# The last addition of each weight conversion: a VectorE instruction replaced by an accumulating transfer that GpSimd issues

## The chip, the cores and the metric

One Trainium2 chip, one core. The metric is the device time of one execution in microseconds (us); lower is better. Besides the times there is a profile: one execution recorded by the hardware profiler. Its engine names are PE (TensorE matmuls), PEld (TensorE weight loads), DVE (VectorE), ACT (ScalarE), POOL (GpSimd) and SP (the queue that issues the kernel's transfers). A line such as L265 is line 265 of the kernel.

## The reference

A gated linear attention over 4 batches, 8 heads, 768 steps and head size 48 keeps a 48x48 state for each head; its output, as 3072 tokens of 384 numbers, goes through a feed-forward layer with 2048 hidden units.

```python
for t in range(S):
    state = alpha[:, :, t, :, None] * state + np.einsum('bhd,bhe->bhde', k[:, :, t], v[:, :, t])
    y[:, :, t] = np.einsum('bhd,bhde->bhe', q[:, :, t], state)
...
h = x @ w_in
g = np.maximum(0.01 * h, h)
return (g @ w_out).astype(np.float32)
```

The weights `w_in` (384x2048) and `w_out` (2048x384) arrive as 64-bit floating point numbers. No engine of the kernel works on those directly; the kernel receives them as 64-bit integers and builds from the bits two 32-bit parts of each weight, HIGH and LOW, whose sum is the weight.

## The kernel before, in words

**Tiling.** The tokens are cut into 24 units of 128 (one batch, 128 steps each); three units make a block of 384 tokens, so there are 8 blocks. The hidden layer is cut into 16 slices f of 128 units. For a block i and a slice f, `ffn_in` (line 485) makes the hidden values with nine matmuls of 128x384 at line 493: for each of three groups of the model dimension HIGH with the high and the low part of the tokens, then LOW with the high part. In a slice the third of the nine matmuls is thus the first that reads LOW weights. ScalarE scales the result by 0.01 (L496), VectorE takes the maximum (L499), ScalarE rounds it (L501) and VectorE subtracts to get the low part (L505). `ffn_out` (line 511) adds to the output with nine more matmuls at L520, three items later (LAG = 3).

**Stages.** First the attention for units 0 to 8, which are blocks 0 to 2 (scans on VectorE, L314 and L320; masks on GpSimd, L367; scalings of the state on GpSimd, L373). Then the feed-forward of blocks 0 and 1, interleaved slice by slice: (block 0, f), (block 1, f), and in the same stretch the weights are converted. From block 2 on the converted weights stay in SBUF, and the rest of the attention is spread between the matmuls.

**Weight conversion.** `load_weights` (L201) loads one slice of both weight matrices into one of four tiles `raw` (128 rows, 768 numbers of 64 bits): one transfer for `w_out` (L213) and four for `w_in` (L209), all issued by SP. `converting(f)` (L226) is a generator that makes HIGH and LOW of slice f in steps, so that its instructions can be placed between others:

- ScalarE scales the top words in place (L245); VectorE shifts and masks them (L248) and joins the sign (L251): the weight cut to 32 bits, in tile `bits`, also called `val` (two buffers).
- ScalarE rounds `val` to the matmul format: HIGH (L254).
- VectorE cuts the power of two out of `bits` into tile `pw` (L258, one buffer), subtracts HIGH from `val` in place (L260), multiplies the low word by 2**-52 and by the power, in place in `pw` (L262), and adds the two into LOW (L265).

**Order.** The program is built by a scheduler that follows dependencies and a simulated timeline and fixes the order of the instructions on each engine's queue; the kernel pins places with "issue after" conditions. Slices 0, 1 and 2 are converted during the attention stage at pinned places. For slices 3 to 15, `put` (L217) fixes one order for VectorE and one for ScalarE across the feed-forward and the conversion: in slice f of block 0 come L248 of slice f+2, then the last step of slice f+1 (L265), then L251 of f+2; around block 1's maximum come L258, L260 and, after L505, L262 of f+2. So the conversion of f+2 is finished during slice f+1.

```python
coming = converting(f + SOON, True)
...
old, new, coming = new or iter(()), coming, converting(f + SOON + 1, True)
gs[n] = ffn_in(i, f, ((), (coming, new, old, new)))
...
gs[n] = ffn_in(i, f, ((new, new), (new,)))
next(new, None)
```

Here `old`, `new` and `coming` are the conversions of slices f+1, f+2 and f+3; each mention is one step. GpSimd issues no transfers in this kernel.

Of the kernel before, what the change touches and what calls it, by code (L numbers as in the profile page):

```python
# [9 lines left out]
F32 = mybir.dt.float32  # L10
F32R = mybir.dt.float32r
I32 = mybir.dt.int32
U32 = mybir.dt.uint32
I64 = mybir.dt.int64
AF = mybir.ActivationFunctionType
ALU = mybir.AluOpType
# [6 lines left out]
def gated_linear_attn_ffn(ctx, tc, q, k, v, alpha, w_in, w_out, out):  # L23
    nc = tc.nc
# [64 lines left out]
    state, vals_sb, rest = rest[:B], rest[B:B + NV], rest[B + NV:]  # L89
# [14 lines left out]
    made = {}  # L104
# [3 lines left out]
    def behind(*key):  # L108

        return tc.issue_after(made[key].ins) if key in made else nullcontext()  # L110
# [106 lines left out]
    def put(ordered, eng, op, *args):  # L217

        if not ordered:
            return op(*args)  # L220
        line = lines[eng]
        with tc.issue_after(line[-1].ins) if line else nullcontext():
            line.append(op(*args))
        return line[-1]

    def converting(f, ordered=False):  # L226

        if f >= NF:
            return
        raw = jobs.pop(f)  # L230
        w_sb[f] = cst.tile([P, 2, 2 * DM], F32R, name=f"w{f}")
        hi, lo = w_sb[f][:, HIGH, :], w_sb[f][:, LOW, :]
        if not f64:
            val = raw[:, :, 0:P].bitcast(F32)
            hi, lo = (t.rearrange("p (g f) -> p g f", f=P) for t in (hi, lo))
            nc.scalar.copy(hi, val)
            made["w", f] = nc.vector.tensor_tensor(lo, val, hi.bitcast(F32), ALU.subtract)
            return
        words = raw.rearrange("p g (f w) -> p (g f) w", w=2)
        top, low = words[:, :, 1], words[:, :, 0]  # L240
        bits = cvp.tile([P, 2 * DM], I32, name="bits", bufs=NBITS)
        val = bits.bitcast(F32)

        with nullcontext() if lines["ACT"] else behind(*AFTER.get(f, ("hi", f - 1))):
            put(ordered, "ACT", lambda: nc.scalar.mul(top.bitcast(F32), top.bitcast(F32), 2.0 ** -112))  # L245
        yield
        with nullcontext() if lines["ACT"] else behind("w", f - 1):
            put(ordered, "DVE", lambda: nc.vector.tensor_scalar(  # L248
                bits, top, 3, 0x7FFFFFF8, ALU.logical_shift_left, ALU.bitwise_and))
        yield  # L250
        put(ordered, "DVE", lambda: nc.vector.scalar_tensor_tensor(  # L251
            bits, top, -0x80000000, bits, ALU.bitwise_and, ALU.bitwise_or))
        yield
        made["hi", f] = put(ordered, "ACT", lambda: nc.scalar.copy(hi, val))  # L254
        yield
        pw = cvp.tile([P, 2 * DM], I32, name="pw", bufs=NPW)
        rest = pw.bitcast(F32)
        put(ordered, "DVE", lambda: nc.vector.tensor_scalar(pw, bits, -0x800000, None, ALU.bitwise_and))  # L258
        yield
        put(ordered, "DVE", lambda: nc.vector.tensor_tensor(val, val, hi.bitcast(F32), ALU.subtract))  # L260
        yield
        put(ordered, "DVE", lambda: nc.vector.scalar_tensor_tensor(  # L262
            rest, low.bitcast(U32), 2.0 ** -52, rest, ALU.mult, ALU.mult))
        yield
        made["w", f] = put(ordered, "DVE", lambda: nc.vector.tensor_tensor(lo, rest, val, ALU.add))  # L265

    def convert(f):
        for _ in converting(f):
            pass
# [284 lines left out]
    for n, _ in enumerate(st):  # L554
        if n == 2:
            load_values(NV - 1)
        while LOADS and LOADS[0][0] in made:
            key, f, part = LOADS.pop(0)
# [8 lines left out]
        if n in STARTS:  # L567
            i, f = items[len(gs)][:2]
# [8 lines left out]
    for n in range(len(items) + LAG):  # L577
        slices = 0
        if n < len(items):
            i, f, slices, _ = items[n]  # L580
            if f == 0:
                if i == 2:
                    st, held = attention(AHEAD, NU), HELD
                while i not in ready:
                    next(st)
                emitted, due = 0, 0.0
            if loaded_f < NF:
                load_weights(loaded_f)
                loaded_f += 1
                if loaded_f == NF:  # L590
                    asked, later = later, None
                    with behind("raw", NF - 1):
                        for fn, *args in asked:
                            fn(*args)
            if n < len(STARTS):
                pass
            elif i == 0:
                if coming is None:
                    coming = converting(f + SOON, True)
                    next(coming)  # L600
                old, new, coming = new or iter(()), coming, converting(f + SOON + 1, True)
                gs[n] = ffn_in(i, f, ((), (coming, new, old, new)))
            elif i == 1:
                gs[n] = ffn_in(i, f, ((new, new), (new,)))
                next(new, None)
            else:
                gs[n] = ffn_in(i, f)
        for half in range(2):
# [5 lines left out]
            if half == 0 and n >= LAG:  # L614
                i, f, _, tag = items[n - LAG]
# [130 lines left out]
```

## Time and profile before

| | |
|---|---|
| Three runs | 530.29, 530.71, 530.88 us; median 530.71 |
| Profiled execution, span from first to last instruction | 530.9 us (no other time of this execution is recorded) |
| Mean granted TensorE clock | 0.994 |
| L265, the last addition | 16 instructions, 15.4 us busy, 960 ns each |
| L262, the multiplication before it | 16 instructions, 15.7 us busy, 978 ns each |
| DMA engines, share of the span | 39.5% in the queue that SP issues to |

How to read the profile: the busy time of an engine is an average over stages with different limits. The "chain of work that ended last" is followed back from the last instruction, at each step to what released it. The view by stage gives the busy time of each engine in a stretch of the span. In the order of time, each line has the start and the length in us, the engine, the line, the operation with its output and inputs and how many instructions were merged, and in brackets the idle time before it with what ended it. A line on transfers gives their number, their size and the median time from issue to landing.

### The profile page before, as it was taken

The numbers are of one execution on the slowest core, as the hardware profiler recorded it, in microseconds if no ns is written. First come the engines' busy times: TensorE is split into PE (matmuls) and PEld (weight loads), VectorE is DVE, ScalarE is ACT, GpSimd is POOL, SyncE is SP. The second block draws the span as 40 slices with busy tenths as digits, with TensorE's granted clock in tenths as the row PEclk, the third lists the DMA queues.
The fourth block names the chain that finished last, engine by engine and source line by source line (L and its number), as shares of the span: only waits on it lengthen the run. The fifth ranks groups of instructions, "written<-read, shape, count | busy, mean of one in ns | idle before, by whom it ended". The sixth has DMA issues, their size and how long they took to land.

```text
span 530.9 us, 9962 instructions
## 1 busy us (share of the span) xinstructions
PE 518.5 (98%) x3778; PEld 500.0 (94%) x3778; DVE 379.0 (71%) x695; ACT 230.7 (43%) x489; POOL 62.6 (12%) x143
## 2 busy tenths in 40 slices
PE   8997999999999999999999999999999999999995
PEld 7886999999999999999999999999999999999995
DVE  6998899999999997777577586585786534333331
ACT  2764855555534444444334444345344444333331
POOL 4554500000000111100101101101010000000000
PEclk9998999999999999999999999999999999999998
DMA  9999975545726533552251431433201000101001
GB/s 144 168 175 170 229 172 133 131 122 141 170 45 184 127 84 81 102 134 49 60 111 30 112 83 44 92 74 86 54 15 25 31 16 1 23 1 44 1 0 51
DMA packets 92982, 46.64 MB, mean 88 GB/s; under 512 B 57856, under 2 KB 90112, under 8 KB 92928
## 3 DMA queue, kind: packets, MB, share of 16 engines
q1 hardware_dynamic: 92928, 45.93, 39.5%
q8 instruction: 32, 0.52, 0.4%
q14 instruction: 22, 0.18, 0.1%
HBM read 38.83 MB, written 4.72 MB: 82 GB/s over the span
## 4 chain that ended last, share of the span: by engine, by line
PE 87%; DVE 7%; DMA 4%; issue 1%; SPq 0%; DVEq 0%; ACT 0%
PE ph L493 35%; PE b L520 32%; PE a L356 4%; PE a L401 3%; PE a L520 3%; DMA small<-in_v_dram 3%; PE a L395 3%; PE a L412 2%; PE b L401 1%; PE a L380 1%; PE b L280 1%; DMA small<-in_alpha_dram 1%; DVE pw L262 1%; DVE gl L505 1%; DVE t L499 1%
## 5 line engine op out<-in xcount | busy, mean ns | idle before, releaser
L493 PE MATMUL ph<-large,w 128*128 128x384 f32 x1152 | 226.6, 338 | 0.5 <-DVE t L499 0.5
L493 PEld LDWEIGHTS ph<-large,w 128*128 128x128 f32 x1152 | 200.1, 188 | 2.8 <-DVE t L499 1.1
L520 PE MATMUL b<-w,gh 128*128 128x384 f32 x672 | 168.9, 340 | 0.0
L499 DVE TENSOR_TENSOR t<-ph,t 128x384 f32<-128x384 f32 x128 | 70.7, 553 | 79.1 <-ACT t L496 78.9
L520 PEld LDWEIGHTS b<-w,gh 128*128 128x128 f32 x672 | 119.4, 188 | 2.1 <-issue 0.4
L496 ACT ACTIVATE t<-ph 128x384 f32<-128x384 f32 x128 | 62.5, 489 | 128.2 <-PE ph L493 128.2
L501 ACT CAST gh<-t 128x384 fp32r<-128x384 f32 x128 | 65.7, 513 | 119.6 <-DVE t L499 119.6
L520 PE MATMUL b<-w,gl 128*128 128x384 f32 x336 | 107.4, 335 | 0.0
L505 DVE TENSOR_TENSOR gl<-t,gh 128x384 fp32r<-128x384 f32 x128 | 70.9, 554 | 34.3 <-ACT gh L501 34.2
L520 PEld LDWEIGHTS b<-w,gl 128*128 128x128 f32 x336 | 62.6, 188 | 0.0
L367 POOL TENSOR_SCALAR_AFFINE_SELECT sm<-sm 128x512 f32<-128x512 f32 x33 | 23.1, 712 | 207.8 <-ACT sm L366 207.8
L356 PEld LDWEIGHTS a<-qs,ks 48*128 48x128 f32 x312 | 24.1, 188 | 5.1 <-issue 4.2
L356 PE MATMUL a<-qs,ks 48*128 48x128 f32 x312 | 28.7, 285 | 0.0
L289 DVE STREAM_TRANSPOSE ks<-small 128x512 f32<-128x512 f32 x15 | 16.7, 1123 | 14.6 <-PE a L380 14.6
L324 POOL COPY pe<-pc 128x4 f32<-128x4 f32 x24 | 4.8, 202 | 163.7 <-DVE pc L314 163.7
L373 POOL TENSOR_TENSOR small<-us,pe 48x192 f32<-48x192 f32 x40 | 22.4, 560 | 1.5
L314 DVE TENSOR_TENSOR_SCAN pc<-e,small 128x128 f32<-128x128 f32 x60 | 20.4, 401 | 0.0
L366 ACT COPY sm<-a 128x512 f32<-128x512 f32 x24 | 14.0, 583 | 14.0 <-PE b L356 12.9
L520 PE MATMUL a<-w,gh 128*128 128x384 f32 x96 | 19.6, 337 | 0.0
L320 DVE TENSOR_TENSOR_SCAN rc<-e,small 128x511 f32<-128x511 f32 x15 | 19.1, 1276 | 0.2
L401 PE MATMUL a<-sm,small 128*48 128x128 f32 x256 | 17.7, 277 | 0.0
L254 ACT CAST w<-bits 128x768 fp32r<-128x768 f32 x16 | 13.4, 838 | 8.4 <-DVE bits L251 7.8
(92 smaller groups left out, 554.4 us busy)
## 6 DMA issues: line engine op xcount, KB each, us to landing
raw<-in_moe_w_out_dram SPq DMA_DIRECT2D x16, 384.0 KB, 3.8
small<-in_v_dram SPq DMA_DIRECT2D x24, 192.0 KB, 3.7
raw<-in_moe_w_in_dram SPq DMA_DIRECT2D x32, 144.0 KB, 4.0
out_dram<-o SPq DMA_DIRECT2D x24, 192.0 KB, 2.0
small<-in_alpha_dram SPq DMA_DIRECT2D x32, 96.0 KB, 2.3
small<-in_q_dram SPq DMA_DIRECT2D x30, 96.0 KB, 2.4
small<-in_k_dram SPq DMA_DIRECT2D x30, 96.0 KB, 2.2
small<-in_alpha_dram SPq DMA_DIRECT2D x30, 80.0 KB, 2.4
```

What stands on the lines that cost most here:

```text
L314: nc.vector.tensor_tensor_scan(pc[:, p, :], aT[:, p, :], ones.broadcast_to([P, C]), 1.0, ALU.mult, ALU.mult)
L320: nc.vector.tensor_tensor_scan(flat[2][:, NP * C - 2::-1], flat[0][:, NP * C - 1:0:-1], flat[1][:, NP * C - 2::-1], last, ALU.mult, ALU.add)
L356: nc.tensor.matmul(ss[s][:, p, :], ks[lo:lo + D, p, :], qs[lo:lo + D, p, :], start=True, stop=True)
L367: made["mask", u] = nc.gpsimd.affine_select(out=sm[s], in_=sm[s], compare_op=ALU.is_ge, fill=0.0, base=0, pattern=[[0, NP], [1, C]], chann ...
L373: nc.gpsimd.tensor_tensor(*scalings.pop(0))
L401: nc.tensor.matmul(y[lo:lo + m, p, :], V[:, c:c + m], masked[u][s][:, p, :], start=not tb and p == 0, stop=p == NP - 1, skip_group_check=True,
L493: nc.tensor.matmul(ph, w_in_of(f, wn, g), xt[:, g, :], start=n == 0, stop=n == 3 * NG - 1)
L496: put(ordered, "ACT", lambda: nc.scalar.mul(t, ph, 0.01))
L499: put(ordered, "DVE", lambda: nc.vector.tensor_tensor(t, ph, t, ALU.max))
L501: put(ordered, "ACT", lambda: nc.scalar.copy(gh, t))
L505: made["gl", i, f] = put(ordered, "DVE", lambda: nc.vector.tensor_tensor(gl, t, gh.bitcast(F32), ALU.subtract))
L520: product = nc.tensor.matmul(po[j], gt[:, js], w_out_of(f, wn), start=f == 0 and n == 0, stop=f == NF - 1 and n == 2)
```

## The change

The last VectorE instruction of the conversion goes. The subtraction writes LOW directly, the multiplication writes into `val`, and a transfer issued by GpSimd adds `val` (in SBUF) to LOW (in SBUF): 128 rows of 768 numbers of 32 bits, 384 KB. The two last VectorE instructions of the conversion keep their shapes but for their output tiles. The generator has one step less; the last step now holds the multiplication and the issue of the transfer, so in the fixed order both come where L262 stood, and the place of L265 stays empty. `made["w", f]`, by which slices 1 and 2 start behind the conversion before, now means the multiplication. That the transfer waits for the multiplication, and the LOW matmuls for the transfer, the scheduler finds from the tiles.

```diff
@@ -254,15 +254,14 @@
         made["hi", f] = put(ordered, "ACT", lambda: nc.scalar.copy(hi, val))
         yield
         pw = cvp.tile([P, 2 * DM], I32, name="pw", bufs=NPW)
-        rest = pw.bitcast(F32)
+        power = pw.bitcast(F32)
         put(ordered, "DVE", lambda: nc.vector.tensor_scalar(pw, bits, -0x800000, None, ALU.bitwise_and))
         yield
-        put(ordered, "DVE", lambda: nc.vector.tensor_tensor(val, val, hi.bitcast(F32), ALU.subtract))
+        put(ordered, "DVE", lambda: nc.vector.tensor_tensor(lo, val, hi.bitcast(F32), ALU.subtract))
         yield
-        put(ordered, "DVE", lambda: nc.vector.scalar_tensor_tensor(
-            rest, low.bitcast(U32), 2.0 ** -52, rest, ALU.mult, ALU.mult))
-        yield
-        made["w", f] = put(ordered, "DVE", lambda: nc.vector.tensor_tensor(lo, rest, val, ALU.add))
+        made["w", f] = put(ordered, "DVE", lambda: nc.vector.scalar_tensor_tensor(
+            val, low.bitcast(U32), 2.0 ** -52, power, ALU.mult, ALU.mult))
+        nc.gpsimd.dma_start(lo, val, accum_op=ALU.add)
 
     def convert(f):
         for _ in converting(f):
```

## The prediction

> **What bounds the kernel now.** I read the page first (engine totals, then the chain that ended last), then the busy time by stage, then the order of time on TensorE and VectorE around the sixteen weight conversions, then the DMA landings.
>
> ```profile
> span 530.9 us, 9962 instructions
> PE 518.5 (98%) x3778; PEld 500.0 (94%) x3778; DVE 379.0 (71%) x695; ACT 230.7 (43%) x489; POOL 62.6 (12%) x143
> PE 87%; DVE 7%; DMA 4%; issue 1%; SPq 0%; DVEq 0%; ACT 0%
> ```
>
> TensorE is busy for 98% of the span and carries 87% of the chain; VectorE carries 7%. So relief of VectorE can only be worth the few places where TensorE waited for it. The stages show where the two are loaded together (columns: stretch, then busy us and instructions of PE, PEld, DVE, ACT, POOL, the granted clock, DMA share, GB/s).
>
> ```profile
> 40.00:50.00 10.00, 6.55 (x78) 5.25 (x77) 9.52 (x18) 5.31 (x12) 6.08 (x8) 0.99 1.26 186
> 50.00:60.00 10.00, 10.00 (x119) 9.27 (x121) 8.47 (x17) 5.95 (x13) 3.22 (x6) 0.84 0.97 179
> 120.00:140.00 20.00, 20.00 (x116) 19.97 (x115) 20.00 (x33) 10.34 (x18) 0.00 (x0) 1.00 0.65 158
> ...
> 129.00:130.00 1.00, 1.00 (x8) 1.00 (x7) 1.00 (x3) 0.45 (x3) 0.00 (x0) 1.00 0.92 345
> ```
>
> The conversions lie in two surroundings. The first three stand in the attention stage, with GpSimd at work and the DMA engines full (share 0.97 and 1.26). The other thirteen stand in the feed-forward stage, where GpSimd does nothing and TensorE and VectorE are both busy all the time. There the question is whether TensorE really runs at its pace or follows VectorE:
>
> ```profile
> 72.89 1.38 PE L493 MATMUL ph<-large,w 128*128 128x384 f32 x7
> ...
> 154.94 1.38 PE L493 MATMUL ph<-large,w 128*128 128x384 f32 x7
> 156.15 0.69 PE L520 MATMUL b<-w,gl 128*128 128x384 f32 x3
> 156.68 1.72 PE L493 MATMUL ph<-large,w 128*128 128x384 f32 x9
> 158.24 1.21 PE L520 MATMUL a<-w,gh 128*128 128x384 f32 x6
> ...
> 163.57 1.86 PE L493 MATMUL ph<-large,w 128*128 128x384 f32 x9 [0.47 <-DVE t L499]
> ```
>
> Nine matmuls take 158.24 - 156.68 = 1.56 us, so one slice f, with its 36 matmuls for two token blocks, needs 6.26 us. The seven matmuls that begin with a slice's LOW weights start at 72.89 for f = 2 and at 154.94 for f = 15: 13 slices in 82.05 us, 6.31 each. TensorE is at its own pace, only 0.67 us above it in all. From 156.68 to 163.57 the same 36 matmuls take 6.89, 0.63 too much, and there the trace names VectorE.
>
> **What the change takes away.** One VectorE addition of 128x768 in each of 16 conversions.
>
> ```profile
> L265 DVE TENSOR_TENSOR w<-pw,bits 128x768 fp32r<-128x768 f32 x16 | 15.4, 960 | 0.0
> PEld a L356 <- DVE w L265: 0.4, 1, 0.4
> ...
> 69.65 0.95 DVE L262 SCALAR_TENSOR_TENSOR pw<-raw,pw 128x768 f32<-128x768 uint32 x1
> ...
> 71.45 0.95 DVE L265 TENSOR_TENSOR w<-pw,bits 128x768 fp32r<-128x768 f32 x1
> 72.32 0.95 DVE L251 SCALAR_TENSOR_TENSOR bits<-raw,bits 128x768 int32<-128x768 int32 x1
> ```
>
> Instructions overlap at their ends, so one addition holds the queue for 72.32 - 71.45 = 0.87 us, 13.9 us in all. Nearly all of that lies beside matmuls. On the path I count the 0.67 us, the 0.63 us and the 0.4 us for which a weight load waited for L265: relief of 1.7 us. The subtraction now writes the LOW weights instead of overwriting its input and the fused multiplication writes the other scratch tile; shapes and count stay, cost nothing.
>
> **What it adds.** After the multiplication, GpSimd issues a transfer of 128 rows of 3,072 B (384 KB) inside SBUF, which also has to read its destination. Before, the LOW weights were ready when L265 ended; now they are ready when this transfer has landed, a time D after the end of the multiplication (L262 of before). No trace shows such a transfer, nor any issued by GpSimd. The nearest rows:
>
> ```profile
> DMA to landing us min/median/max: 3.4/4.0/6.5
> ...
> raw<-in_moe_w_out_dram SPq DMA_DIRECT2D x9, 384.0 KB, 3.5
> raw<-in_moe_w_in_dram SPq DMA_DIRECT2D x18, 144.0 KB, 3.9
> raw<-in_moe_w_in_dram SPq DMA_DIRECT2D x20, 48.0 KB, 3.6
> ...
> raw<-in_moe_w_out_dram SPq DMA_DIRECT2D x6, 384.0 KB, 5.6
> ...
> raw<-in_moe_w_out_dram SPq DMA_DIRECT2D x1, 384.0 KB, 9.1
> ...
> SPq L213 <- DVE pw L262: 33.4, 10, 3.7
> ```
>
> The first line is for the copies inside SBUF (line 449, 144 KB); the w_out rows are loads as large as the new transfer: 3.5 us in the stretch 72 to 156 us, 5.6 in 40 to 72 us, and 9.1 for the one issued in 42 to 44 us. So D lies between 3.4 and 9.1. The last line matters for the thirteen quiet conversions: the load of the next raw slice waits for the same multiplication (ten times), so its burst of 768 KB (w_out, and two w_in loads of 144 KB and two of 48 KB) starts at the very moment at which the new transfer is issued. At the 345 GB/s of 129 to 130 us that burst lasts 2.3 us, and the second read of 384 KB costs 1.1. I take 3.5 + 1.1 for the second read + 1.2 for half of the burst: D = 5.8 us. In the full attention stage 5.6 holds the crowding already, so D = 5.6 + 1.1 = 6.7.
>
> The Trainium skill ("DMA: Bandwidth & Descriptors", section on the anatomy of one DMA on the gpsimd path) fits such a transfer at about 2.0 us plus its bytes over 436 GB/s. By it D would be an estimated 2.9 us, less than the 3.5 us that this trace shows for a plain load of that size; with it the result would be that of the faster rival below.
>
> **Does D fit, thirteen times?** One slice near the end:
>
> ```profile
> 137.82 1.72 PE L493 MATMUL ph<-large,w 128*128 128x384 f32 x9
> ...
> 148.61 1.38 PE L493 MATMUL ph<-large,w 128*128 128x384 f32 x7
> ...
> L496 ACT ACTIVATE t<-ph 128x384 f32<-128x384 f32 x128 | 62.5, 489 | 128.2 <-PE ph L493 128.2
> ...
> 143.38 0.55 DVE L499 TENSOR_TENSOR t<-ph,t 128x384 f32<-128x384 f32 x1
> 143.85 0.95 DVE L260 TENSOR_TENSOR bits<-bits,w 128x768 f32<-128x768 f32 x1
> ...
> 145.18 0.95 DVE L262 SCALAR_TENSOR_TENSOR pw<-raw,pw 128x768 f32<-128x768 uint32 x1
> ```
>
> The nine matmuls of block 1, slice 12, end at 137.82 + 1.56 = 139.38. Their maximum runs on VectorE only at 143.38: VectorE is 4 us late. With 0.87 us less in each slice it catches up, and the maximum follows the matmuls by ScalarE's scaling (L496, 489 ns) and a hand-over, some 0.6. From the maximum's start to the multiplication's end are 145.18 + 0.95 - 143.38 = 2.75 us, so the multiplication for slice 14 could end at 139.38 + 3.35 = 142.7. The LOW weights of slice 14 are wanted at 148.61: 5.9 us. With D = 5.8 the cover just holds. If it is gone, the excess recurs every second slice, because slice f + 2 hangs on slice f: (D - 5.9) / 2 for each of 13.
>
> **Does D fit, the first three times?**
>
> ```profile
> 47.69 1.25 DVE L262 SCALAR_TENSOR_TENSOR pw<-raw,pw 128x768 f32<-128x768 uint32 x1
> ...
> 59.98 0.94 DVE L262 SCALAR_TENSOR_TENSOR pw<-raw,pw 128x768 f32<-128x768 uint32 x1
> ...
> 46.93 2.38 POOL L373 TENSOR_TENSOR small<-us,pe 48x192 f32<-48x192 f32 x2
> ...
> 61.35 2.85 POOL L367 TENSOR_SCALAR_AFFINE_SELECT sm<-sm 128x512 f32<-128x512 f32 x2 [3.35 <-ACT sm L366]
> 64.18 1.32 POOL L373 TENSOR_TENSOR small<-us,pe 48x192 f32<-48x192 f32 x2
> ...
> 55.23 1.47 PE L493 MATMUL ph<-large,w 128*128 128x384 f32 x7
> ...
> 65.44 1.50 PE L493 MATMUL ph<-large,w 128*128 128x384 f32 x7
> ```
>
> Slice 0: the multiplication ends at 48.94, GpSimd is free at 49.31, the LOW weights are wanted at 55.23: 5.9 us for D = 6.7, late by 0.8. Slice 1: end 60.92, a removed addition earlier makes it 60.05, wanted at 65.44: 5.4 us, late by 1.3. Slice 2: end 70.60, two additions earlier 68.86, wanted at 72.89: 4.0 us for D = 5.8, late by 1.8. A stall pushes all later work of TensorE, so these don't add: 0.8, then 0.5, then 0.5 more, 1.8 in all. Queued behind the waiting transfer on GpSimd are the masks (L367) and state scalings (L373), for which TensorE's second attention products wait; in slice 1 GpSimd is idle until 61.35, so issued at 60.05 the transfer delays nothing.
>
> TensorE's idle time can also cost clock: in 40 to 50 us it idles 3.45 us, and in 50 to 60 us the granted clock is 0.84, 1.6 us of full pace lost. After the 0.47 us idle at 163.57 I find no such loss. My three stalls, 0.5 to 0.8 each, are nearer to the short one: I charge nothing and leave 1.6 us to the range.
>
> **The sum.** 530.9 - 1.7 + 1.8 = 531.0 on the span. The three runs have a median of 530.71, 0.2 below the span, the only time that this execution has; so 530.8.
>
> **Rivals.**
> Late in every slice (slower): the burst takes the whole share, D = 5.8 + 1.2 = 7.0. It decides from D = 5.9 on. Then (7.0 - 5.9) / 2 x 13 = 7.2, the early stalls end at 3.0, the relief is 1.7: +8.5, 539.2. For it speaks the collision behind L262; against it that the rows of the burst are shorter pieces, which should let the other queue through. Chance 0.22.
>
> Held up by VectorE (slower): GpSimd finishes its issue only when a VectorE instruction lets it. The trace shows the two engines stretching each other:
>
> ```profile
> 64.22 0.90 DVE L248 TENSOR_SCALAR bits<-raw 128x768 int32<-128x768 int32 x1 [1.09 <-ACT raw L245]
> 70.98 0.55 DVE L248 TENSOR_SCALAR bits<-raw 128x768 int32<-128x768 int32 x1
> ```
>
> The same instruction takes 0.90 us beside GpSimd's L373 and 0.55 alone. If the issue waits for one such instruction (0.55), D = 6.35 and 7.25 early: 0.45 / 2 x 13 = 2.9, early stalls 2.4, relief 1.7: +3.6, 534.3. This is the Trainium skill's rule that speaks against the change ("SBUF — State Buffer", the "DVE blocks DMA" trap): a DMA that GpSimd issues needs it to write descriptors, from which a VectorE instruction in a two-port mode locks it out. Nothing here shows a descriptor written so. Chance 0.06.
>
> Behind the masks (slower): if slice 1's transfer is queued after L373, it is issued at 65.50 instead of 60.05 and wanted at 65.44: late by 6.7, relief 1.7, +5.0, 535.7. The order on GpSimd's queue is set when the program is built; the multiplication ending before 61.35 speaks against. Chance 0.09.
>
> All hidden (faster): D = 4.0 or less, the median of the SBUF copies. No stall, relief alone: 529.0. Against it: loads of that size took 5.6 us in the attention stage. Chance 0.18.
>
> Nothing gained: GpSimd's issue stretches a VectorE instruction by 0.35 each (5.6 of 13.9 us given back) or an unseen wait replaces the relief: 530.7. Chance 0.07.
>
> **Numbers.** The forecast's case has 0.38; its own range is that of D half a us shorter or longer: shorter leaves early stalls of 1.3 and gives 530.3; longer costs 0.4 / 2 x 13 = 2.6 in the slices and 2.3 early and gives 533.9. From it 0.26 stay within 0.2% of before (1.1 us, about what a measurement of this kernel can tell), 0.10 are slower, 0.02 faster. So faster 0.18 + 0.02 = 0.20; same 0.26 + 0.07 = 0.33; slower 0.22 + 0.06 + 0.09 + 0.10 = 0.47. Both signs hold much of the chance, so the range is wider than the forecast's own: from all hidden, 529.0, to late in every slice with half of the clock's loss, 540.0.
>
> **What would show it.** Right: 16 GpSimd transfers landing 5 to 7 us after the multiplication; in 72 to 156 us VectorE near 86% busy (6.3 - 0.87 of each 6.3 us) and TensorE at 6.26 us per slice; the wait at 163.57 gone; new waits of TensorE for the transfer only at 55, 65 and 73 us. Wrong: TensorE waiting in slices 3 to 15 (D too small in my sum), no wait at all (D too large), or VectorE still full in 72 to 156 us.

## The result, and the profile after

| | before | after |
|---|---|---|
| Runs compared | 530.29 to 531.85 us, four | 545.06 to 547.81 us, four |
| Median | 530.80 us | 545.78 us |
| Ratio, with its 95% interval | | 1.0287 [1.0264, 1.0311] |
| Profiled execution, span | 530.9 us | 543.5 us (its time: 545.38) |

The change costs 15 us; the prediction had no change, and a range that ended at 540.0. In the changed kernel the numbers of the lines move: L262 is still the multiplication, L260 the subtraction, **L264** the transfer; the hidden matmuls are L492, ScalarE's scaling L495, the maximum L498, the rounding L500, the subtraction for the low part L504, the output matmuls L519.

First the page of the changed kernel, span, engine totals and the chain:

```profile
span 543.5 us, 10008 instructions
PE 520.1 (96%) x3778; PEld 498.2 (92%) x3778; DVE 366.6 (67%) x679; ACT 231.6 (43%) x489; POOL 76.2 (14%) x159
PE 79%; DMA 12%; DVE 5%; SPq 1%; issue 1%; ACT 1%; DVEq 0%; ACTq 0%; POOLq 0%
```

VectorE is 12.4 us lighter (379.0 to 366.6); the prediction had counted 13.9 for the removed additions. TensorE does the same 3778 matmuls in 1.6 us more, but is idle for 23.4 us of the span instead of 12.4: 11.0 of the 12.6 us by which the span grew are idle TensorE. In the chain DMA went from 4% to 12%: by the lines of the page the raw loads have 7%, most of it ahead of 90 us, and the transfer 3%. The list of waits names the transfer:

```profile
PEld ph L492 <- DMA w<-bits: 13.7, 9, 2.4
PE ph L492 <- DMA w<-bits: 11.2, 8, 2.3
```

(Columns: total us, times, longest.) TensorE waited 11.2 us, in eight places, for LOW weights that had not landed. By stretch (columns as in the prediction):

```profile
60.00:70.00 10.00, 7.70 (x72) 7.33 (x71) 6.28 (x12) 7.16 (x15) 2.19 (x4) 1.00 1.05 246
70.00:80.00 10.00, 8.60 (x50) 8.28 (x49) 5.91 (x10) 3.06 (x5) 1.73 (x2) 1.00 1.05 214
100.00:120.00 20.00, 18.10 (x103) 17.46 (x101) 16.43 (x28) 10.33 (x18) 2.56 (x3) 1.00 0.71 174
120.00:140.00 20.00, 17.60 (x99) 17.28 (x100) 14.48 (x24) 9.51 (x17) 2.58 (x3) 1.00 0.72 172
```

Between 120 and 140 us both engines were full before (20.00 and 20.00); now TensorE works 17.60 and VectorE 14.48 of the 20. The freed VectorE time turned into waiting. In order of time, TensorE's waits for the transfer in slices 1, 2, 3, 6 and 8:

```profile
67.02 1.50 PE L492 MATMUL ph<-large,w 128*128 128x384 f32 x7 [2.30 <-DMA w<-bits]
78.44 3.34 PE L492 MATMUL ph<-large,w 128*128 128x384 f32 x16 [1.40 <-DMA w<-bits]
83.71 1.48 PE L492 MATMUL ph<-large,w 128*128 128x384 f32 x7 [0.69 <-DMA w<-bits]
...
106.69 2.70 PE L492 MATMUL ph<-large,w 128*128 128x384 f32 x14 [1.38 <-DMA w<-bits]
...
120.89 2.74 PE L492 MATMUL ph<-large,w 128*128 128x384 f32 x14 [1.42 <-DMA w<-bits]
```

The other three are 1.44 us at 92.54, 1.51 at 135.24 and 1.03 at 148.82: 4.4 us in slices 1 to 3, and 6.8 us in every second slice from 4 to 12. The group after a wait also starts slower. From 106.69 to the start of the next group at 109.23 the 14 matmuls take 2.54 us, at 1.56 / 9 each they would take 2.43; the 16 at 78.44 take 3.26 instead of 2.77. Over the eight groups that is 1.3 us. (The lengths in the lines are longer, since the last matmul of a group overlaps the next group: 16 matmuls without a wait are listed with 2.94 us, at 98.55.)

So waits of 11.2 us and slow restarts of 1.3 come to 12.5 us, close to the 12.6 us between the spans. It is no closed account, for the profiled execution of before has a loss of its own that the other has not (its granted clock of 0.84 in 50 to 60 us). Of the other 2.4 of the 15 us between the medians some 1.9 come from which execution was profiled: 17 runs of the kernel before on another chip have a median span of 529.4 us, 1.5 under the profiled one, and the profiled execution of after is 0.4 us under its median.

Why every second slice, is seen in the loop from one wait to the next. The transfer, the raw load that the same multiplication releases, and VectorE in between (slice 6 of blocks 0 and 1, conversion of slice 8):

```profile
108.74 0.56 DVE L498 TENSOR_TENSOR t<-ph,t 128x384 f32<-128x384 f32 x1 [2.22 <-ACT t L495]
109.21 0.55 DVE L248 TENSOR_SCALAR bits<-raw 128x768 int32<-128x768 int32 x1
109.80 0.96 DVE L251 SCALAR_TENSOR_TENSOR bits<-raw,bits 128x768 int32<-128x768 int32 x1
110.67 0.55 DVE L504 TENSOR_TENSOR gl<-t,gh 128x384 fp32r<-128x384 f32 x1
111.14 0.55 DVE L258 TENSOR_SCALAR pw<-bits 128x768 int32<-128x768 int32 x1
111.61 0.55 DVE L498 TENSOR_TENSOR t<-ph,t 128x384 f32<-128x384 f32 x1
112.08 0.95 DVE L260 TENSOR_TENSOR w<-bits,w 128x768 fp32r<-128x768 f32 x1
112.94 0.55 DVE L504 TENSOR_TENSOR gl<-t,gh 128x384 fp32r<-128x384 f32 x1
113.41 0.95 DVE L262 SCALAR_TENSOR_TENSOR bits<-raw,pw 128x768 f32<-128x768 uint32 x1
114.43 0.35 SPq L213 DMA_DIRECT2D raw<-in_moe_w_out_dram  x1
114.66 0.85 POOL L264 DMA_DIRECT2D w<-bits  x1 [6.99 <-DVE bits L262]
```

The transfers between 98 and 142 us, beside the loads of the next raw slices that SP issues then:

```profile
raw<-in_moe_w_out_dram SPq DMA_DIRECT2D x6, 384.0 KB, 3.7
w<-bits POOLq DMA_DIRECT2D x6, 384.0 KB, 6.1
raw<-in_moe_w_in_dram SPq DMA_DIRECT2D x12, 144.0 KB, 5.0
```

LOW of slice 6 starts at 106.69. Block 0's maximum follows after 2.05 us, block 1's after 2.87 more, because VectorE has L248, L251, L504 and L258 between them; the multiplication ends 2.75 us after that (114.36), GpSimd starts 0.30 later, and its transfer lands 6.2 us after the issue, at 120.86. LOW of slice 8 starts at 120.89. That is 14.2 us for two slices whose 72 matmuls need 12.5. Slices 7, 9 and so on hang on the odd ones before them and had some slack. The last four transfers have no raw load beside them: those of slices 12 and 13 land after 5.2 and 5.3 us beside loads of the attention, those of 14 and 15 after 4.3 and 3.9. Behind slice 12 the waits end.

**The theory to test:** the loop multiplication, transfer, LOW matmuls, maximum, multiplication is 1.7 us too long, since VectorE's order gives the transfer less room than I counted, and because the transfer collides with the raw loads. **Rivals:** the loss is in the three early slices, which push everything; the accumulating transfer is slow by itself; the GpSimd queue has a price of its own; the raw loads, slowed by the transfers, hold the conversions up. On the last the trace of the changed kernel already speaks: ScalarE's first step of a conversion (L245) waits for a raw load five times, 3.6 us in all, the last time at 71.33. So this can touch the early slices, not the waits of slices 4 to 12.

### The profile page after: what moved, and what is told of

Same layout as the page of the kernel before. It is cut to its first block, busy times and chain, and to the rows that moved or that the text cites. A ratio compares the mean times of both kernels' runs of the same rounds, so it can differ in the third digit from the quotient of the medians.

```text
span 543.5 us, 10008 instructions
## 1 busy us (share of the span) xinstructions
PE 520.1 (96%) x3778; PEld 498.2 (92%) x3778; DVE 366.6 (67%) x679; ACT 231.6 (43%) x489; POOL 76.2 (14%) x159
## 4 chain that ended last, share of the span: by engine, by line
PE 79%; DMA 12%; DVE 5%; SPq 1%; issue 1%; ACT 1%; DVEq 0%; ACTq 0%; POOLq 0%
PE ph L492 32%; PE b L519 30%; DMA raw<-in_moe_w_in_dram 5%; PE a L355 4%; DMA w<-bits 3%; PE a L400 3%; PE a L394 2%; PE a L519 2%; DMA raw<-in_moe_w_out_dram 2%; PE a L411 1%; PE a L379 1%; DMA large<-large 1%; PE b L279 1%; PE b L400 1%; DVE bits L262 1%
## 5 line engine op out<-in xcount | busy, mean ns | idle before, releaser
L492 PE MATMUL ph<-large,w 128*128 128x384 f32 x1152 | 226.2, 339 | 11.2 <-DMA w<-bits 11.2
L492 PEld LDWEIGHTS ph<-large,w 128*128 128x128 f32 x1152 | 199.8, 188 | 16.0 <-DMA w<-bits 13.7
L519 PE MATMUL b<-w,gh 128*128 128x384 f32 x672 | 169.1, 340 | 0.0
L498 DVE TENSOR_TENSOR t<-ph,t 128x384 f32<-128x384 f32 x128 | 70.6, 551 | 99.3 <-ACT t L495 99.1
L495 ACT ACTIVATE t<-ph 128x384 f32<-128x384 f32 x128 | 62.7, 490 | 166.9 <-PE ph L492 166.9
L519 PEld LDWEIGHTS b<-w,gh 128*128 128x128 f32 x672 | 119.4, 188 | 2.3 <-ACT gh L500 0.4
L500 ACT CAST gh<-t 128x384 fp32r<-128x384 f32 x128 | 65.7, 514 | 100.9 <-DVE t L498 100.9
L519 PE MATMUL b<-w,gl 128*128 128x384 f32 x336 | 107.4, 335 | 0.0
L504 DVE TENSOR_TENSOR gl<-t,gh 128x384 fp32r<-128x384 f32 x128 | 70.4, 550 | 35.8 <-ACT gh L500 34.8
L519 PEld LDWEIGHTS b<-w,gl 128*128 128x128 f32 x336 | 62.6, 188 | 0.0
L264 POOL DMA_DIRECT2D w<-bits x16 | 14.6, 915 | 91.5 <-DVE bits L262 76.3
L519 PE MATMUL a<-w,gh 128*128 128x384 f32 x96 | 19.9, 336 | 0.0
L365 ACT COPY sm<-a 128x512 f32<-128x512 f32 x24 | 14.0, 582 | 13.8 <-PE b L355 12.6
L519 PEld LDWEIGHTS a<-w,gh 128*128 128x128 f32 x96 | 17.0, 188 | 0.0
```

The source lines that it names most:

```text
L492: nc.tensor.matmul(ph, w_in_of(f, wn, g), xt[:, g, :], start=n == 0, stop=n == 3 * NG - 1)
L495: put(ordered, "ACT", lambda: nc.scalar.mul(t, ph, 0.01))
L498: put(ordered, "DVE", lambda: nc.vector.tensor_tensor(t, ph, t, ALU.max))
L500: put(ordered, "ACT", lambda: nc.scalar.copy(gh, t))
L504: made["gl", i, f] = put(ordered, "DVE", lambda: nc.vector.tensor_tensor(gl, t, gh.bitcast(F32), ALU.subtract))
L519: product = nc.tensor.matmul(po[j], gt[:, js], w_out_of(f, wn), start=f == 0 and n == 0, stop=f == NF - 1 and n == 2)
```

## The experiments

Each measured time is a median; the kernel before ran on the same chip (531.12 us beside the first four experiments, 17 runs; 530.63 beside the middle four, 9 runs; 531.19 beside the last four, 7 runs).

**1 and 2. The early slices alone, the others alone.** The last addition goes back to VectorE for the slices that are left out:

```diff
-        put(ordered, "DVE", lambda: nc.vector.tensor_tensor(lo, val, hi.bitcast(F32), ALU.subtract))
+        if f >= 3:
+            put(ordered, "DVE", lambda: nc.vector.tensor_tensor(lo, val, hi.bitcast(F32), ALU.subtract))
+            yield
+            made["w", f] = put(ordered, "DVE", lambda: nc.vector.scalar_tensor_tensor(
+                val, low.bitcast(U32), 2.0 ** -52, power, ALU.mult, ALU.mult))
+            nc.gpsimd.dma_start(lo, val, accum_op=ALU.add)
+            return
...
+        made["w", f] = put(ordered, "DVE", lambda: nc.vector.tensor_tensor(lo, rest, val, ALU.add))
```

For the second, the condition is `f < 3`.

> Only slices 3 to 15 use the transfer; 0 to 2 keep the VectorE addition. Loop theory (each transfer lies on a loop of two slices: LOW matmuls of slice f, block 0's maximum, the conversion of f+2 on VectorE, the transfer, LOW matmuls of f+2; 14.2 us instead of 12.5): the six stalls after slice 3 stay, 7.5 us of idle TensorE and some 0.2 each of refilling it, 8.7, and 1.9 us outside the span; the stalls of slices 1 and 2 (2.3 and 1.4) go: 541 to 542 us. Rival, early theory (the loss is made in the attention stage, where the DMA engines are full, and only handed on): near 533. Rival, slow loads (the transfers slow the raw loads and these hold the conversions up): 541 too, but TensorE would wait for conversions whose ScalarE step waits for a load.

> Only slices 0 to 2 use the transfer. Loop theory: slices 3 to 15 run at the pace of before; stalls at slices 1 and 2 of 2.3 and 1.4 us with some 0.4 of refilling, and 1.9 outside the span, less what VectorE catches up meanwhile (at most 1.3): 535 to 537 us. Early theory: most of the 15 us, 540 or more.

Measured: thirteen transfers 542.76 us (542.01 to 544.21), ratio 1.0227 [1.0203, 1.0251]; the first three alone 538.09 us (537.03 to 538.56), ratio 1.0123 [1.0101, 1.0145]. Both parts cost, and both a little more than expected (by 0.8 and 1.1 us). They don't add: 11.6 + 7.0 is more than the 15.0 of the whole. One reason shows on TensorE. In the kernel with the first three alone:

```profile
79.63 4.55 PE L500 MATMUL ph<-large,w 128*128 128x384 f32 x16 [2.58 <-DMA w<-bits]
...
80.00:82.00 2.00, 2.00 (x7) 2.00 (x7) 0.00 (x0) 0.00 (x0) 0.00 (x0) 0.50 1.03 236
```

Sixteen matmuls take 4.55 us; without a wait 16 are listed with 2.94, and behind the changed kernel's shorter wait of 1.40 with 3.34. After the idle time of 2.58 us the granted clock is 0.50 (the last line, by stretch). The thirteen alone had the same at 81.96 (idle 2.43, 14 matmuls in 4.10 instead of 2.70 us, clock 0.50 in 82 to 84). The early slices are thus worth 3.3 us (the whole less the thirteen) to 7.0 (alone), not 1.8, and where the first wait is long, it is paid again in clock.

The loop is there without the early slices. With the thirteen alone the waits are shorter, but odd and even slices both have them: from the wait at 104.19 to the one at 118.17, two slices on, are 13.98 us, from 111.02 to 125.25 14.23.

**3. A copy in place of the accumulation.**

```diff
-        nc.gpsimd.dma_start(lo, val, accum_op=ALU.add)
+        nc.gpsimd.dma_start(lo, val)
```

> The transfer copies instead of accumulating (LOW is then only the small product, the computation is changed there), so that the destination isn't read: 3,072 B pieces should take the 0.12 us of plain ones instead of 0.25. Loop theory: eight pieces per DMA engine save 1.0 us, landing 6.1 to about 5.1 us, loop 14.2 to 13.1, excess per slice 0.83 to 0.3, 13 x 0.5 = 7 us and 1 to 2 early: 537 to 539 us. Rival, issue and hand-over dominate (GpSimd's 0.86 us and a fixed cost, the second read is hidden): landing stays at 6, 544 to 546 us.

Measured 541.66 us (540.24 to 543.01), ratio 1.0188 [1.0165, 1.0211]. Median landing between 98 and 142 us:

```profile
w<-bits POOLq DMA_DIRECT2D x7, 384.0 KB, 5.3
```

0.8 us less than with the accumulation, and some 4 us off the time, between my two expectations. I had expected more of both, since I took the second read to cost a full microsecond; the direction holds. With no raw load beside it, the last copy lands after 2.6 us, the last accumulating transfer after 3.9. The accumulation is one part of the length, not the largest.

**4. The kernel before with one transfer by GpSimd** (the store of one of the 24 output tiles), to see whether the GpSimd queue costs something by being used at all:

```diff
-            nc.sync.dma_start(out[r:r + P, :], o)
+            (nc.gpsimd if i == 4 and j == 0 else nc.sync).dma_start(out[r:r + P, :], o)
```

> The kernel before, with one of its 24 output stores issued by GpSimd instead of SP. The changed kernel's time is 1.9 us longer than its span, where before the two agree. If this is a fixed price of having any transfer on GpSimd's queue: 532.6 us with a span of 530.8. If it comes with each accumulating transfer (16 of them): 530.8 to 531.

Measured 531.59 us, ratio 1.0007 [0.9996, 1.0017]: no such price. What had looked like one, that the runs of the changed kernel last about 1.9 us longer than their spans, is there in the kernel before too (1.7 us in its runs here).

**5. One slice further ahead.** The conversion of f + 3 instead of f + 2 runs in slice f; slice 3 is converted in one lump before the feed-forward.

```diff
-    SOON, EARLY = 2, 3
+    SOON, EARLY = 3, 3
...
+                    for _ in converting(EARLY, True):
+                        pass
```

> The changed kernel with the conversions of slices 4 to 15 one slice further ahead (three instead of two; slice 3 is converted in one piece at the start of the ordered part). Loop theory: the loop now spans three slices, 18.8 us of matmuls against 14.2 of waiting; no stall after slice 4, but a lump of some 4 us of VectorE work at the start, of which a few us may show: 535 to 539 us. Slow loads: a raw tile is wanted one slice earlier, so no better or worse, 545 to 550.

Measured 540.53 us (539.86 to 540.87), ratio 1.0180 [1.0162, 1.0198], just outside what I expected. In its stretches:

```profile
100.00:120.00 20.00, 20.00 (x117) 20.00 (x117) 18.85 (x30) 10.59 (x19) 3.11 (x3) 1.00 0.79 191
120.00:140.00 20.00, 20.00 (x117) 20.00 (x116) 18.57 (x30) 11.03 (x20) 3.16 (x4) 1.00 0.85 202
```

TensorE is full again, although the transfers are as long as before (median 5.9 us). So the waits of slices 4 to 12 are a matter of room, as the loop says. Its loss lies ahead of 84 us: waits of 1.53 and 2.53 us for the transfer and 2.06 us for VectorE, busy with the lump, and a granted clock of 0.50 from 78 to 82.

**6. The multiplication ahead of block 1's maximum.**

```diff
-                gs[n] = ffn_in(i, f, ((new, new), (new,)))
-                next(new, None)
+                gs[n] = ffn_in(i, f, ((new, new, new, new), ()))
```

> The changed kernel with the end of the conversion (subtraction, multiplication, issue) ahead of block 1's maximum on VectorE instead of behind it. The transfer is the same, it only starts earlier in the loop: from block 0's maximum to the multiplication's end 4.7 us instead of 5.6. Loop theory: 13.3 us for two slices instead of 14.2, 0.45 less per slice, 6 us in all: 540 us. Slow loads or full DMA engines: the work of the DMA engines is the same, 545 to 546.

Measured 547.03 us (543.34 to 550.13), ratio 1.0294 [1.0244, 1.0344]: a miss. The loop did get shorter (from 110.46 to 123.87, 13.4 us), and TensorE worked 55.73 us of 80 to 140 instead of 53.56. But a wait of 3.27 us at 81.17 was followed by slow matmuls, and 140 to 160 us held 17.75 us of work instead of 18.97. This order delays block 1's output; the experiment moves too much at once to speak for or against.

**7. The raw loads held back** until the transfer has landed (a GpSimd instruction reads LOW and touches the raw tile):

```diff
+        if f >= EARLY:
+            nc.gpsimd.tensor_copy(raw.bitcast(F32)[:, 0, 0:1], lo[:, 0:1].bitcast(F32))
```

> The changed kernel, and for slices 3 to 15 GpSimd copies one column of LOW into the raw tile when the transfer has landed, so that the next load into that tile starts after the transfer instead of together with it (the copied numbers are never used). Loop theory with the collision as the reason for D: landing 6.1 to 4.2 us as for the last two slices, where nothing else was loaded; the loop comes to 12.3 us, below the 12.5 of the matmuls, no stall after slice 3: 535 to 537 us. If the collision is not the reason: landing stays near 6, 545 to 547. Slow loads: the loads start 4 to 6 us later, longer still, above 548.

Measured 545.16 us (543.23 to 548.94), ratio 1.0295 [1.0261, 1.0330], landings of 5.8 us: inconclusive. As a landing takes about a slice, the held load only moved to the next transfer's issue (released at 111.28, loads issued at 111.50, next transfer at 111.80). The collision was not removed; experiment 9 removes it.

**8. GpSimd adds by an instruction**, for slices 3 to 15 (the others as in experiment 1):

```diff
-            nc.gpsimd.dma_start(lo, val, accum_op=ALU.add)
+            nc.gpsimd.tensor_tensor(lo, lo.bitcast(F32), val, ALU.add)
```

> Slices 3 to 15: GpSimd adds in place as an instruction of its own instead of issuing the transfer (slices 0 to 2 as before). At 0.56 us for 192 numbers a row the addition should take some 2.2 us, against 6.4 from multiplication to landing. Loop theory: 7.7 + 2.4 = 10.1 us, below 12.5, no stall, and no fixed cost outside the span; VectorE is relieved: 529 to 530.5 us. Rival, the two engines stretch each other (0.3 us on VectorE instructions beside GpSimd's): VectorE stays full, 530.5 to 533.

Measured 540.96 us (540.42 to 541.62), ratio 1.0194 [1.0177, 1.0210], against an expectation of a small gain. GpSimd's addition is short, but VectorE pays for it:

```profile
103.84 1.86 POOL L265 TENSOR_TENSOR w<-w,bits 128x768 fp32r<-128x768 f32 x1 [5.10 <-DVE bits L263]
104.15 1.97 DVE L248 TENSOR_SCALAR bits<-raw 128x768 int32<-128x768 int32 x1
```

```profile
100.00:120.00 20.00, 19.54 (x106) 17.66 (x105) 19.93 (x27) 10.32 (x18) 5.57 (x3) 1.00 0.40 107
```

L248 takes 1.97 us instead of 0.55 and ends 0.42 us after GpSimd does. VectorE is full again (19.93 of 20) with a slice of 6.96 us, 0.70 over TensorE's pace, 9.1 us in thirteen slices. TensorE follows: its weight loads wait 8.0 us in 15 places for the maximum. 1.42 us of stretching against 0.87 saved. The Trainium skill ("SBUF — State Buffer", section on the two sides of SBUF) says that a VectorE instruction in a two-port mode and one of GpSimd exclude each other for the whole length of the one that starts first; this row agrees, though it doesn't show the mode. So the addition was not to be had from GpSimd's own lanes either.

**9. No collision with loads.** From slice 7 on nothing but one row of `w_out` is loaded, and the raw tile of four slices before is converted again.

```diff
+        if f >= 7:
+            jobs[f] = kept[f] = kept[f - NRAW]
+            made["raw", f] = nc.sync.dma_start(jobs[f].bitcast(I64)[0:1, NG:], w_out[f * P:f * P + 1, :].rearrange("p (g f) -> p g f", g=NG))
+            return
```

> From slice 7 on nothing but one row of w_out is loaded (the conversion works on the raw tile of four slices before once more), so the weights of slices 7 to 15 are wrong and their transfers have no load of 768 KB beside them. Loop theory, with the collision as the reason for the long landing: landings fall from 6.1 us to about 4.2 from the transfer of slice 7 on, the loop of two slices from 14.2 us to about 12.3, under the 12.5 us of matmuls, so TensorE stops waiting after 100 us: 6 to 8 us less than the changed kernel, 538 to 540. Rival, the accumulating transfer is slow by itself: landings stay at 6 us, the waits stay, 545 to 546.

Measured 540.11 us (538.54 to 540.91), ratio 1.016 [1.012, 1.020]: as the collision theory expected. Between 98 and 142 us, landings, then TensorE:

```profile
w<-bits POOLq DMA_DIRECT2D x7, 384.0 KB, 4.2
```

```profile
100.00:120.00 20.00, 20.00 (x115) 19.49 (x114) 17.54 (x30) 10.83 (x20) 2.82 (x4) 1.00 0.95 196
120.00:140.00 20.00, 20.00 (x117) 19.96 (x116) 17.96 (x29) 11.54 (x22) 3.08 (x3) 1.00 0.37 68
```

Two of the seven had loads of the attention beside them, which come earlier in this kernel, with the DMA engines at 0.93 between 102 and 118 us; they landed after 4.6 and 4.9 us. So it is mostly the raw loads, issued together with the transfer, that make the 6.1.

With 4.2 us instead of 6.1 the loop is 14.2 - 1.9 = 12.3 us, under the 12.5 of the matmuls, and no wait for the transfer is left after 91.43. The loss that remains is made ahead of that (waits of 4.3 us, and a granted clock of 0.50 between 68 and 70). The order on VectorE was unchanged. So two things are needed for the loss in the slices: a landing of 6 us and a short room.

**10. Twelve transfers, one slice further ahead.** As in experiment 5, but the first four slices are wholly VectorE's.

> The conversion of slices 4 to 15 by transfer and one slice further ahead; slices 0 to 3 wholly by VectorE, slice 3 in one lump before the feed-forward. Loop theory: no wait for a transfer anywhere, since each has a slice more than it needs; what is left is the lump of some 5 us on VectorE, of which 0 to 4 us show: 531 to 535, against 530.9 of the kernel before. Rival, the transfer costs something even where TensorE does not wait for it: 538 or more.

Measured 538.32 us (537.68 to 539.33), ratio 1.0134 [1.0097, 1.0171]. The number is the rival's, the cause is not:

```profile
75.93 3.25 PE L500 MATMUL ph<-large,w 128*128 128x384 f32 x9 [5.23 <-DVE t L506]
```

This is TensorE's only wait between 50 and 190 us: the lump shows with 5.23 us, and the nine matmuls behind it take 3.25 us instead of 1.72, at a granted clock of 0.50. That is 6.8 of the 7.1 us. The twelve transfers, landing after 6.0 us, cost TensorE nothing. They gain nothing either: TensorE was at its own pace in these slices before.

**11 and 12. The first steps of the next conversion ahead of block 0's maximum**, so that L248 and L251 no longer stand between the two maxima; with all sixteen transfers, and with slices 3 to 15 alone.

```diff
-                gs[n] = ffn_in(i, f, ((), (coming, new, old, new)))
+                gs[n] = ffn_in(i, f, ((coming, new, old, new), ()))
```

> The changed kernel with only the order on VectorE altered: L248 and L251 of slice f + 2 go ahead of block 0's maximum instead of behind it, so that they no longer stand between block 0's and block 1's maximum, on which the multiplication and the transfer follow. Loop theory: from one LOW group to the next but one 12.8 us instead of 14.2, excess 0.15 instead of 0.83 us per slice: 8 to 9 us less than the changed kernel, 537 to 538. Rival, the length of the transfer alone sets the loss: 545 to 546.

> The same altered order with the addition of slices 0 to 2 on VectorE as before, transfers only for slices 3 to 15. Loop theory: 542.8 of the thirteen transfers in the old order less 7 to 9 us: 534 to 536. Rival, the length of the transfer alone sets the loss: 542 to 543.

Measured: 542.23 us (541.78 to 544.48), ratio 1.0217 [1.0175, 1.0259], and 541.70 us (538.86 to 542.02), ratio 1.0180 [1.0134, 1.0225]. The first is a part of what I expected, the second hardly differs from experiment 1's 1.0227 [1.0203, 1.0251] and decides nothing. The loop of the first, on TensorE and VectorE:

```profile
120.32 3.04 PE L492 MATMUL ph<-large,w 128*128 128x384 f32 x16 [0.43 <-DMA w<-bits]
133.63 3.04 PE L492 MATMUL ph<-large,w 128*128 128x384 f32 x16 [0.47 <-DMA w<-bits]
```

```profile
122.36 0.56 DVE L498 TENSOR_TENSOR t<-ph,t 128x384 f32<-128x384 f32 x1 [0.51 <-ACT t L495]
123.56 0.56 DVE L504 TENSOR_TENSOR gl<-t,gh 128x384 fp32r<-128x384 f32 x1 [0.63 <-ACT gh L500]
124.03 0.56 DVE L258 TENSOR_SCALAR pw<-bits 128x768 int32<-128x768 int32 x1
124.50 0.55 DVE L498 TENSOR_TENSOR t<-ph,t 128x384 f32<-128x384 f32 x1
```

The loop is 13.3 us instead of 14.2: the maxima are 2.14 us apart instead of 2.87, not 1.4, because L504 now waits 0.63 us for ScalarE's rounding. The transfer was as long as ever (6.0 us), and the waits of the slices fell to about 0.45 but for one of 1.38 at 107.10. So the order on VectorE carries part of the loss, as experiment 9 showed for the loads. Another part of the expected gain was lost early: at 78.38 TensorE waits 3.20 us (1.40 in the changed kernel; the wait ends at the same time in both), and its 14 matmuls then take 3.92 us, with a granted clock of 0.50 in 80 to 82.

## Why the prediction was wrong, point by point

**The bound, right.** TensorE sets the pace, and relief of VectorE could only be worth the few waits for it. In experiments 5 and 10 VectorE has time left and TensorE is full as before.

**The relief of 1.7 us, of no consequence.** VectorE's time fell nearly as counted (12.4 of 13.9 us). What I counted on the path was overtaken by the waits for the transfer.

**The failed step: the cover of 5.9 us.** It rests on "the maximum follows the matmuls by ScalarE's scaling and a hand-over, some 0.6". I let VectorE catch up by the time that it saves and so put block 1's maximum 0.6 us behind its matmuls, as if the order on its queue did not hold it back. From the start of the LOW matmuls to block 1's maximum I thus had 3.9 us (3.29 us of TensorE and 0.6). It measures 4.92 (106.69 to 111.61), although TensorE had done those matmuls by 109.23: L248, L251, L504 and L258, with block 0's maximum itself 2.87 us, are queued ahead of block 1's. The other piece, maximum to end of the multiplication, is 2.75 us as predicted. The cover is 12.52 - 2.05 - 2.87 - 2.75 = 4.85 us. I had quoted the queue's order in the description of the kernel and did not walk through it.

**The term that was mis-sized: D.** Predicted 5.8 us from the end of the multiplication, measured 0.3 + 6.1 = 6.4. Term by term: for the hand-over to GpSimd I had nothing, it takes 0.3; for the plain transfer 3.5, the last one of experiment 3 took 2.6; for the second read 1.1, it costs 1.3 (3.9 - 2.6; 0.8 beside the loads); for half of the burst 1.2. That the loads start with the transfer and lengthen it was right in kind: 4.2 us without them (experiment 9), 6.1 with them, so 1.9 us for the burst. With my own rule, (D - cover) / 2 for each of 13, the right D alone would give (6.4 - 5.9) / 2 x 13 = 3.3 us, the right cover alone (5.8 - 4.85) / 2 x 13 = 6.2, both 10.1. Measured are 6.8 us of waits in slices 4 to 12. The transfers of the last four slices have no burst beside them, which the rule did not know; for the nine slices 4 to 12 it gives (6.4 - 4.85) / 2 x 9 = 7.0.

**The early slices.** I took D = 6.7 for the first two and 5.8 for the third; they landed 5.3, 8.1 and 6.7 us after their issue. Slice 0 was not late, where I had 0.8; slice 1 was late by 2.30 (I had 1.3), then slice 2 by 1.40. That is 3.7 us instead of 1.8, and slice 3 adds 0.69. For slice 2 the start was wrong too. I let its multiplication end two removed additions earlier, at 68.86; it ended at 71.43, 0.83 later than before, for the conversion begins with ScalarE's step:

```profile
64.46 0.56 DVE L248 TENSOR_SCALAR bits<-raw 128x768 int32<-128x768 int32 x1 [3.65 <-ACT raw L245]
```

Before, L248 started at 64.22. VectorE had the time free and could not use it. The 9.1 us of one load in that stage, which I quoted and left to the range, was nearer for slice 1 than the median.

**The clock.** I charged nothing for it. In the changed kernel the clock stays at 1.00 in the four stretches shown, so that was right here; in experiments 1, 2, 10 and 11 the granted clock fell to 0.50 at one long wait, and the matmuls behind it took 1.3 to 1.6 us more than at pace.

**The rivals.** Late in every slice (539.2, chance 0.22) named the right place, every second slice as I had argued, but not the right term: the measured D of 6.4 lies between my 5.8 and its 7.0, and the cover, which it shared with the forecast, was a microsecond too long. Against it I had put that the rows of the burst are shorter pieces. Half of the burst, the w_out load, has rows of 3,072 B (384 KB in 128 rows) like the transfer. Held up by VectorE: GpSimd is busy 0.85 to 0.88 us with most issues, also with L248 beside it (the issue at 86.47, L248 at 86.56 in 0.55 us). But the issues of slices 12 and 14 take 1.23 and 1.22 us, and both end 0.08 to 0.09 us after an L248 that ran in their second half:

```profile
143.54 1.23 POOL L264 DMA_DIRECT2D w<-bits  x1 [7.18 <-PE ph L492]
...
144.13 0.55 DVE L248 TENSOR_SCALAR bits<-raw 128x768 int32<-128x768 int32 x1
```

So the Trainium skill's "DVE blocks DMA" trap ("SBUF — State Buffer") fits two of the sixteen issues, at some 0.37 us each; it is no cause of the loss. Behind the masks: no, slice 1's transfer was issued at 58.87, ahead of them. All hidden needed D = 4.0 or less, which is about what a transfer takes without loads beside it. The fit of the Trainium skill ("DMA: Bandwidth & Descriptors"), 2.9 us, is under the 3.9 us of the shortest landing; the plain copies of experiment 3 landed after 2.6 to 8.1 us.

**The time outside the span.** I took the median as 0.2 below the profiled execution's time, having taken the span for its time. A run lasts 1.7 to 2.0 us longer than its span in all kernels here; the span of before that was profiled, with its clock of 0.84 in one stretch, was a long one, and the two errors nearly cancelled. That was luck.

**What stays open.** Why landings in the attention stage spread from 5.3 to 8.3 us; and whether a version with slice 3 converted early without a lump would be level with the kernel before. It was not tried. By experiment 10 it could be level, and nothing here says that it could be faster.

## What to carry to other kernels

Moving work off an engine that is not the bound gains at most the waits that the bound has for it; moving it to a transfer puts a landing of several microseconds into every chain that goes through it. Before doing so, find the loop that goes through the transfer, write down the order of each queue in it instruction by instruction, and compare its length with the time that the bound needs for the same work. A load that is released by the same instruction as the transfer will run beside it: take the landing from a stretch where both run.

## What the runs showed of the hardware

- An accumulating transfer inside SBUF of 384 KB lands 3.9 to 4.3 us after its issue with no loads beside it (slices 14 and 15, and experiment 9 from 118 us on), 6.1 beside the raw loads, and 5.3 to 8.3 in the attention stage and just behind it. In the trace of the changed kernel one of its pieces of 3,072 B takes 253 ns in the median of 2,048; in the plain copy of experiment 3 the same pieces take 138. The Trainium skill ("Collectives: The Full Stack", why ReduceScatter is half of AllGather) explains the half rate of an addition by DMA in a collective by its two source reads; the ratio of 1.8 here is near that.
- An idle time of TensorE of 2.1 to 2.6 us was followed by matmuls at about half pace for some 3 us in several kernels (16 in 4.55 us instead of 2.94 after 2.58 us in experiment 2; 7 in 2.57 instead of 1.50 after 2.38 us in experiment 9), with a granted clock of 0.50. The 2.30 us at 67.02 in the changed kernel was not (7 in 1.50, clock 1.00). The Trainium skill ("TensorE: Matmul & The Clock Gate", Part 1, on the clock gate) has the clock fall after an idle window of about 3.4 us; here shorter ones were enough at times.
- A GpSimd addition of 128x768 takes 1.86 us and stretches VectorE's L248 beside it from 0.55 to 1.97 us. The issue of a transfer by GpSimd left L248 at 0.55 in the changed kernel; where L248 ran in the middle of the issue, in experiments 5 and 10, it took up to 0.67 and 0.72 us and the issue 1.03.
